# Attention and two MoE layers: the first part's order counts changes of TensorE's tiling, and the last tokens' step runs on column halves

## The chip, the cores and the metric

The kernel runs on one core of one Trainium2 chip. Its time is the device time of one execution, in microseconds. The engines are TensorE (PE; its weight loads are listed apart as PEld), VectorE (DVE), ScalarE (ACT), GpSimd (POOL) and the queue that issues most DMAs (SP).

## The reference

Three stages follow each other, all in 32-bit floating point. The first is attention by random features, for 4 batches of 8 heads with 576 tokens of 64 numbers; the second a dense layer pair over all 2304 tokens; the third a layer pair with 8 experts, of which each token takes one.

```python
def phi(x):                       # omega: 128 features of 64 numbers
    proj = einsum('bhsd,md->bhsm', x, omega)
    h = proj - sum(x * x, -1) / 2
    return exp(h - max(h)) / sqrt(128)
q_p, k_p = phi(q * scale), phi(k * scale)
kv = einsum('bhsm,bhsd->bhmd', k_p, v)
z = sum(k_p, axis=2)
attn = einsum('bhsm,bhmd->bhsd', q_p, kv) / (einsum('bhsm,bhm->bhs', q_p, z) + 1e-6)

x = attn, as 2304 tokens of 512
h = x @ w_in                      # 512 to 2048
x = max(0.01 * h, h) @ w_out      # 2048 to 512

expert = argmax(cosine(x, expert_emb) / tau)
out = gate * (max(x @ w1[expert], 0) @ w2[expert])
```

## The kernel before

The attention works on 16 pairs of heads. A pair has 2 x 512 tokens that fill the partitions four at a time, and the last 64 tokens of each head, which stand together as one tile of 128 partitions (the letter m in names). For each pair a chain of some 50 named steps runs over the engines. Its PE steps are:

- Tk, Tm, Tq: transposes of k, of the last tokens and of q (L516), on the full array.
- Pk, Pq: projections to features, one matmul for each head and tile, on 64 rows each: the array is tiled in two row halves (L532, form 64*128). Pm is the projection of the last tokens on the full array (L542).
- KVm, KV0, KV1: sums over tokens of features times values, one bank of PSUM (kv) for all three. The 128 features go out as two column halves of 64 (L597 and L607, form 128*64). KVm starts the sum with the last tokens; KV0 and KV1 add to it, in either order.
- F0, F1, Fm: transposes of q's features (L622, L626), full array.
- U0, U1: numerators and denominators, on column halves (L642; the last tokens at the end of U1, L649).
- XT: the finished x back into columns, four transposes (L688), full array. Xm: the same for the last tokens (L692), below.

Between them ACT, the DVE and POOL copy, square, take maxima and exponentials. After U0 and U1 the DVE's step dn (L661 to L664) takes the reciprocals of nine denominators, xs0 and xs1 (L671) divide, and xs1 also makes xm for the last tokens (L678). Of these, partitions 0 to 63 belong to one head and 64 to 127 to the other. The kernel before writes xm as 128 x 128 with zeros in the half that is the other head's: the multiply at L664 puts the reciprocal beside a zero, by a 0/1 mask named own, and L678 multiplies both copies. Xm then is one matmul of xm with two, the folded identity (both 64-column halves of the identity added up), made once at the start on POOL (L435 to L440).

As soon as pairs 0 to 3 are done, the dense layer's first group of five chunks (GROUPS[0], M1 and M2, L759 to L761 and L800 to L802) begins on the finished tokens, in blocks of 256, and fills PE beside the later pairs. The weights' conversion (steps C0 to CL) runs on the DVE, ACT and POOL beside it.

The order of all these steps, on every engine and in SP's queue of loads, is not left to the framework: issue_order plays the first part through in a small model, in which each entry of STEPS has, for each engine that could do it, a duration and a rank, its use of PSUM banks (+ takes, - gives back) and the steps before it. The rank of a step of pair i is its own plus RANK[0] times i (dense steps: RANK[2]). Where an engine is free, the step that can start first is taken, and among those that can start then, the one of lowest rank. The resulting list is emitted as it stands. Behind it, from the last attention step on, the framework orders the rest. BUSY is only the model's view of PE's clock.

Of the kernel before, what the change touches and what calls it, by code (L numbers as in the profile page):

```python
# [110 lines left out]
    "ylm": ("p", (("V", 0.14, 55.3),), "-xm", "yhm"),  # L111
# [21 lines left out]
}  # L133
RANK = (949.6, 44297.0, 875.5)
# [7 lines left out]
BUSY = {"KV0": 0.5, "KV1": 0.5, "KVm": 0.6, "U0": 0.5, "U1": 0.5}  # L142
# [3 lines left out]
def issue_order(dense):  # L146
# [41 lines left out]
    free["P"] = WARM  # L188

# [14 lines left out]
    while len(order) < len(waits):  # L204
# [6 lines left out]
        for e, steps in open_.items():  # L211
            at = {}
            for s in steps:
                at[s] = max(ready[s][e], free[e])
                b = kind_of_room(s)
                if b:
                    at[s] = max(at[s], spot(b)[0])
            soon = min(at.values(), default=math.inf)
            if soon < first:
                first, late = soon, soon + AHEAD[e]  # L220
                pick = min((rank[e, *s], s, e) for s in steps if at[s] <= late)[1:]
# [14 lines left out]
        if e == "P":  # L236
            work, dur = dur, 0.0
# [26 lines left out]
def tile_attention_moe_moe(  # L264
# [159 lines left out]

    v1s = [atp.tile([P, 5, 2, D + 2], F32, name=f"v1s{j}", tag=f"v1{j}") for j in range(2)]
    dns = [atp.tile([P, 11], F32, name=f"dn{j}", tag=f"dn{j}") for j in range(2)]
    xms = [atp.tile([P, P], F32, name=f"xm{j}", tag=f"xm{j}") for j in range(2)]
# [6 lines left out]

    own = atp.tile([P, 2], F32, name="own", tag="own")  # L435
    G.memset(own, 0.0)
    for h in range(2):
        G.memset(own[h * 64 : h * 64 + 64, h : h + 1], 1.0)
    two = atp.tile([P, D], F32, name="two", tag="two")
    G.tensor_tensor(two, ident[:, 0:D], ident[:, D:P], op=ALU.add)  # L440
# [160 lines left out]
    def kv(i, j):  # L601

        f = st[i].pop(f"fk{j}")
        for h in range(2):
            for a in range(2):
                for c in HALVES:
                    PE.matmul(  # L607
                        st[i]["kv"][c, h, :], f[:, 2 * h + a, c], vs[i][:, 2 * a + j, h, 0 : D + 1],
                        start=False, stop=(h == 1 and a == 1 and "kv_" in st[i]),
                    )  # L610
        st[i]["kv_"] = j
# [45 lines left out]
    def dens(i):  # L657


# [3 lines left out]
        V.reciprocal(dn[:, 0:9], dn[:, 0:9])  # L663
        V.tensor_scalar_mul(dn[:, 9:11], own, dn[:, 8:9])  # L664

    def ratio(i, j):
# [10 lines left out]
        if j == 1:  # L677
            V.tensor_tensor(  # L678
                xms[i % 2].rearrange("p (h d) -> p h d", h=2),
                u_view(i, 1)[:, 4:5, 0:D].to_broadcast([P, 2, D]),  # L680
                dn[:, 9:11].unsqueeze(2).to_broadcast([P, 2, D]), op=ALU.mult,
            )
# [34 lines left out]
    def on(f, *args):  # L717
        return lambda i, e: f(i, *args)
# [877 lines left out]
```

## Time and profile before

| | us |
|---|---|
| median of 3 runs | 835.98 (835.43 to 838.81) |
| the profiled execution | 839.26 |
| its span, first to last instruction | 837.5 |
| PE busy | 780.6 (93%) |
| DVE busy | 529.4 (63%) |
| ACT busy | 342.3 (41%) |
| POOL busy | 312.2 (37%) |
| granted clock of PE, mean | 0.980 |

The shares are means over parts that differ: the first part is attention with dense work beside it, then follow the rest of the dense layers and the experts. Busy time of PE counts matmuls from start to a modelled end, and they overlap; where the text below speaks of the cost of a step, it therefore goes from the start of one instruction to the start of the next.

### The profile page before, as it was taken

How to read it: one execution, taken by the hardware profiler on the slowest of the kernel's cores; microseconds unless marked ns; L12 is line 12 of the kernel's file. 1: busy time of each engine (PE TensorE's matmuls, PEld its weight loads, DVE VectorE, ACT ScalarE, POOL GpSimd, SP SyncE). 2: the span in 40 equal slices, each digit the busy share in tenths (PEclk: the TensorE clock that was granted, in tenths of full speed). 3: DMA queues.
4: the chain of work that ended last, by engine and by line, in shares of the span. 5: the costliest groups of instructions: out<-in, count | busy, mean ns of one | idle time of the engine just before them, and what ended most of it. 6: DMA issues, size and time to landing. Idle time of an engine off the chain costs nothing. (4 is left out here: it accounts for less than half of the span.)

```text
span 837.5 us, 15718 instructions
## 1 busy us (share of the span) xinstructions
PE 780.6 (93%) x5722; PEld 684.4 (82%) x5722; DVE 529.4 (63%) x1282; ACT 342.3 (41%) x878; POOL 312.2 (37%) x445
## 2 busy tenths in 40 slices
PE   7998999999999999999999999796978999998992
PEld 6776788888898999999989889675857789997992
DVE  6999987877465477253869789988894222222121
ACT  5885755766374444233333433542441211112110
POOL 5766543311064454244342443654562101111000
PEclk9999999999999999999999999898999899999997
DMA  5555423210263266351123412684631201111000
GB/s 157 158 137 139 136 75 102 62 41 16 76 228 129 76 217 220 131 190 36 55 46 45 47 39 39 213 124 117 67 99 26 66 26 53 51 51 51 26 26 31
DMA packets 68318, 75.85 MB, mean 91 GB/s; under 512 B 32691, under 2 KB 49148, under 8 KB 68094
## 3 DMA queue, kind: packets, MB, share of 16 engines
q1 hardware_dynamic: 64766, 65.19, 29.4%
q0 software_dynamic: 3456, 9.49, 3.7%
q8 instruction: 48, 0.79, 0.4%
q14 instruction: 48, 0.39, 0.2%
HBM read 55.65 MB, written 19.00 MB: 89 GB/s over the span
## 5 line engine op out<-in xcount | busy, mean ns | idle before, releaser
L320 POOL TENSOR_TENSOR glo<-gg,ghi 128x384 fp32r<-128x384 f32 (+1 forms) x97 | 101.6, 1048 | 185.2 <-ACT ghi L311 173.8
L759 PE MATMUL ph<-xb,ring 128*128 128x384 f32 (+1 forms) x444 | 142.0, 320 | 0.6 <-DVE ring L311 0.5
L760 PE MATMUL ph<-xb,ring 128*128 128x384 f32 (+1 forms) x444 | 140.2, 316 | 1.3 <-DVE ring L320 1.2
L761 PE MATMUL ph<-xb,ring 128*128 128x384 f32 (+1 forms) x444 | 140.6, 317 | 0.0
L934 DVE CUSTOM_DVE_ANT_0 jv<-xl,en 128x512 bf16<-128x512 f32 x144 | 124.9, 890 | 1.3
L800 PE MATMUL px<-ring,ghi 128*128 128x512 f32 x288 | 115.8, 402 | 7.3 <-ACT ghi L311 6.5
L801 PE MATMUL px<-ring,ghi 128*128 128x512 f32 x288 | 115.2, 400 | 0.2 <-DVE ring L320 0.2
L802 PE MATMUL px<-ring,glo 128*128 128x512 f32 x288 | 113.5, 402 | 1.3 <-POOL glo L320 1.3
L769 DVE SCALAR_TENSOR_TENSOR gg<-hs 128x384 f32<-128x384 f32 (+1 forms) x111 | 65.3, 589 | 75.9 <-ACT hs L311 71.1
L311 ACT CAST ghi<-gg 128x384 fp32r<-128x384 f32 (+1 forms) x104 | 49.0, 472 | 105.0 <-DVE gg L769 97.7
L759 PEld LDWEIGHTS ph<-xb,ring 128*128 128x128 f32 x444 | 84.1, 189 | 5.9 <-DVE ring L311 1.0
L760 PEld LDWEIGHTS ph<-xb,ring 128*128 128x128 f32 x444 | 84.0, 189 | 5.8 <-DVE ring L320 1.9
L761 PEld LDWEIGHTS ph<-xb,ring 128*128 128x128 f32 x444 | 84.1, 189 | 0.3
L1212 DVE SCALAR_TENSOR_TENSOR fh<-fh,fh 128x256 fp32r<-128x256 f32 x48 | 20.4, 425 | 90.6 <-ACT fh L1211 90.6
L311 ACT COPY hs<-ph 128x384 f32<-128x384 f32 (+1 forms) x101 | 44.0, 438 | 79.0 <-PE ph L761 76.2
L800 PEld LDWEIGHTS px<-ring,ghi 128*128 128x128 f32 x288 | 55.0, 191 | 16.9 <-ACT ghi L311 7.5
L802 PEld LDWEIGHTS px<-ring,glo 128*128 128x128 f32 x288 | 54.8, 192 | 14.7 <-POOL glo L320 2.8
L1211 ACT ACTIVATE fh<-fh 128x256 fp32r<-128x256 f32 x48 | 18.4, 384 | 112.8 <-PE fh L1205 112.7
L801 PEld LDWEIGHTS px<-ring,ghi 128*128 128x128 f32 x288 | 54.9, 191 | 9.0 <-DVE ring L320 0.5
L1278 POOL DMA_INDIRECT out_dram<-ot,xg x14 | 14.1, 1008 | 123.8 <-DVE ot L1277 79.5
L1203 PE MATMUL fh<-xth,w 128*128 128x256 f32 x128 | 35.8, 282 | 0.0
L1204 PE MATMUL fh<-xth,w 128*128 128x256 f32 x128 | 35.8, 281 | 0.0
(1085 smaller groups left out, 1743.5 us busy)
## 6 DMA issues: line engine op xcount, KB each, us to landing
xl<-xpart SPq DMA_DIRECT2D x36, 256.0 KB
rawi<-in_moe_w_in_dram SPq DMA_DIRECT2D x16, 512.0 KB
rawo<-in_moe_w_out_dram SPq DMA_DIRECT2D x16, 512.0 KB
rws<-in_moe_w_dram SPq DMA_DIRECT2D x16, 512.0 KB
xpart<-xo SPq DMA_DIRECT2D x18, 256.0 KB
xpart<-xl SPq DMA_DIRECT2D x18, 256.0 KB
xs<-xl SPq DMA_DIRECT2D x18, 256.0 KB
k<-in_k_dram SPq DMA_DIRECT2D x16, 256.0 KB
```

The source lines that it names most:

```text
L311: (A.copy if e == "A" else ENG[e].tensor_copy)(out_, in_)
L320: eng.tensor_tensor(lo, src, hi.bitcast(F32), op=ALU.subtract)
L759: PE.matmul(ph, wh, xb[blk][:, 0, kk, d], start=(kk == 0), stop=False)
L760: PE.matmul(ph, wl, xb[blk][:, 0, kk, d], start=False, stop=False)
L761: PE.matmul(ph, wh, xb[blk][:, 1, kk, d], start=False, stop=(kk == 3))
L769: V.scalar_tensor_tensor(gs["gg"], gs["hs"], 0.01, gs["hs"], op0=ALU.mult, op1=ALU.max)
L800: PE.matmul(px, ghi[:, d], r[:, 2, :], start=first, stop=False)
L801: PE.matmul(px, ghi[:, d], r[:, 3, :], start=False, stop=False)
L802: PE.matmul(px, glo[:, d], r[:, 2, :], start=False, stop=last)
L934: V.tensor_tensor_reduce(out=jv, in0=xfin[t], in1=rt["en"][:, e, :], scale=1.0, scalar=0.0, op0=ALU.mult, op1=ALU.add, accum_out=lg[:, j, ...
L1203: PE.matmul(ph, wh, xh, start=(kk == 0), stop=False)
L1204: PE.matmul(ph, wl, xh, start=False, stop=False)
```

## The change

All durations that a change of tiling had been mixed into are stated anew in STEPS, all ranks are others, and the order counts a change of tiling. KVm is no step of its own any more: it is issued at the head of KV0, and KV1 comes after KV0. Xm multiplies xm, now 128 x 64 without zeros, by the two column halves of the identity, each into its own 64 partitions of PSUM; own, two and the multiply at L664 go. Below, "..." stands for lines left out; every other line of STEPS has a new rank too.

```diff
-    "Lv": ("p", (("D", 2.5, 3363.9),), "", "KVm-2 KV0-2 KV1-2"),
+    "Lv": ("p", (("D", 2.5, -319.5),), "", "KV1-2"),
...
-    "Pk": ("p", (("P", 0.95, -1038.8),), "++pk", "xk"),
+    "Pk": ("p", (("P", 0.88, -1341.2),), "++pk", "xk"),
...
-    "Pq": ("p", (("P", 0.95, 693.6),), "++pq", "xq"),
+    "Pq": ("p", (("P", 0.88, 430.8),), "++pq", "xq"),
...
-    "KVm": ("p", (("P", 0.17, 521.8),), "+kv", "em Lv"),
-    "KV0": ("p", (("P", 0.7, -393.5),), "", "ek0 KVm"),
-    "KV1": ("p", (("P", 0.7, -489.4),), "", "ek1 KVm"),
-    "kf": ("p", (("A", 0.17, -142.9), ("V", 0.2, -1171.9)), "-kv", "KV0 KV1 U0-2 U1-2"),
+    "KV0": ("p", (("P", 0.69, -1008.2),), "+kv", "em Lv ek0"),
+    "KV1": ("p", (("P", 0.465, 162.4),), "", "ek1 KV0"),
+    "kf": ("p", (("A", 0.17, -686.0), ("V", 0.2, -1724.5)), "-kv", "KV1 U0-2 U1-2"),
...
-    "U0": ("p", (("P", 0.7, 1578.8),), "+u0", "fc0 kf"),
-    "U1": ("p", (("P", 0.85, -170.1),), "+u1", "fc1 fcm kf"),
-    "dn": ("p", (("V", 0.63, -194.0),), "", "U0 U1"),
+    "U0": ("p", (("P", 0.465, 1675.4),), "+u0", "fc0 kf"),
+    "U1": ("p", (("P", 0.58, 1455.6),), "+u1", "fc1 fcm kf"),
+    "dn": ("p", (("V", 0.46, 230.8),), "", "U0 U1"),
...
-    "xs1": ("p", (("V", 0.54, 1132.4),), "-u1", "dn XT-2 Xm-2"),
-    "XT": ("p", (("P", 0.44, -1465.1),), "+xt", "xs0 xs1"),
-    "Xm": ("p", (("P", 0.22, -3129.3),), "+xm", "xs1"),
+    "xs1": ("p", (("V", 0.47, 1587.0),), "-u1", "dn XT-2 Xm-2"),
+    "XT": ("p", (("P", 0.44, -1008.5),), "+xt", "xs0 xs1"),
+    "Xm": ("p", (("P", 0.116, -1036.3),), "+xm", "xs1"),
...
-    "M1": ("d", (("P", 1.4, -2103.9),), "+h", ""),
+    "M1": ("d", (("P", 1.4, 1419.6),), "+h", ""),
...
-    "M2": ("d", (("P", 1.38, 2123.8),), "+x", "GL"),
+    "M2": ("d", (("P", 1.38, 3751.0),), "+x", "GL"),
...
-RANK = (949.6, 44297.0, 875.5)
+RANK = (1003.0, 87777.0, 642.4)
...
-BUSY = {"KV0": 0.5, "KV1": 0.5, "KVm": 0.6, "U0": 0.5, "U1": 0.5}
+BUSY = {}
+
+HALVED = {"Pk": 1, "Pq": 1, "KV0": 2, "KV1": 2, "U0": 2, "U1": 2, "Xm": 2}
+CHANGE = 0.17
+SAME = 738.7
...
+    half = 0
...
-                pick = min((rank[e, *s], s, e) for s in steps if at[s] <= late)[1:]
+                pick = min(
+                    (rank[e, *s] - SAME * (e == "P" and HALVED.get(s[0], 0) == half), s, e)
+                    for s in steps if at[s] <= late
+                )[1:]
...
         if e == "P":
-            work, dur = dur, 0.0
+            work, dur = dur, CHANGE * (HALVED.get(name, 0) != half)
+            half = HALVED.get(name, 0)
...
-    dns = [atp.tile([P, 11], F32, name=f"dn{j}", tag=f"dn{j}") for j in range(2)]
-    xms = [atp.tile([P, P], F32, name=f"xm{j}", tag=f"xm{j}") for j in range(2)]
+    dns = [atp.tile([P, 9], F32, name=f"dn{j}", tag=f"dn{j}") for j in range(2)]
+    xms = [atp.tile([P, D], F32, name=f"xm{j}", tag=f"xm{j}") for j in range(2)]
...
-    own = atp.tile([P, 2], F32, name="own", tag="own")
-    G.memset(own, 0.0)
-    for h in range(2):
-        G.memset(own[h * 64 : h * 64 + 64, h : h + 1], 1.0)
-    two = atp.tile([P, D], F32, name="two", tag="two")
-    G.tensor_tensor(two, ident[:, 0:D], ident[:, D:P], op=ALU.add)
...
     def kv(i, j):
 
+        if j == 0:
+            kv_last(i)
         f = st[i].pop(f"fk{j}")
...
-                        start=False, stop=(h == 1 and a == 1 and "kv_" in st[i]),
+                        start=False, stop=(h == 1 and a == 1 and j == 1),
...
-        V.reciprocal(dn[:, 0:9], dn[:, 0:9])
-        V.tensor_scalar_mul(dn[:, 9:11], own, dn[:, 8:9])
+        V.reciprocal(dn, dn)
...
         if j == 1:
-            V.tensor_tensor(
-                xms[i % 2].rearrange("p (h d) -> p h d", h=2),
-                u_view(i, 1)[:, 4:5, 0:D].to_broadcast([P, 2, D]),
-                dn[:, 9:11].unsqueeze(2).to_broadcast([P, 2, D]), op=ALU.mult,
-            )
+            V.tensor_scalar_mul(xms[i % 2], u_view(i, 1)[:, 4, 0:D], dn[:, 8:9])
...
-        PE.matmul(ps[:, 0:D], xms[i % 2], two, start=True, stop=True)
+        for c in HALVES:
+            PE.matmul(ps[c, 0:D], xms[i % 2], ident[:, c], start=True, stop=True)
```

## Rows read from the trace of the kernel before

**Rows 1.** Busy time by stretch: stretch, busy us (instructions) of each engine, PE clock, DMA

```profile
20.00:112.00 92.00, 83.35 (x1036) 69.57 (x1032) 89.67 (x219) 67.33 (x214) 57.58 (x106) 1.00 0.50 136
112.00:220.00 108.00, 107.42 (x1315) 92.55 (x1315) 84.06 (x241) 66.28 (x213) 26.75 (x58) 1.00 0.19 55
220.00:500.00 280.00, 279.83 (x1507) 251.65 (x1506) 176.24 (x370) 113.57 (x246) 113.37 (x119) 1.00 0.39 115
500.00:838.00 338.00, 294.47 (x1714) 257.85 (x1712) 166.04 (x418) 85.01 (x183) 103.26 (x97) 0.95 0.29 66
```

**Rows 2.** PE in order of time (start, us, line, operation): first and last change

```profile
8.91 1.01 PE L532 MATMUL pj0k<-om_bd,x0k 64*128 64x128 f32 x5
...
215.91 0.50 PE L800 MATMUL px<-ring,ghi 128*128 128x512 f32 x1
```

**Rows 3.** PE in order of time, around a projection that stands alone

```profile
114.89 0.40 PE L801 MATMUL px<-ring,ghi 128*128 128x512 f32 x1
115.12 0.40 PE L802 MATMUL px<-ring,glo 128*128 128x512 f32 x1
115.45 1.16 PE L532 MATMUL pj7q<-om_bd,x7q 64*128 64x128 f32 x16
116.54 0.66 PE L516 MATMUL tr11k<-ident,k 128*128 128x128 f32 x4
```

**Rows 4.** PE in order of time: a U step alone, two projections together

```profile
189.00 0.69 PE L642 MATMUL u<-kvf,qT 128*64 128x65 f32 x16
189.61 0.66 PE L516 MATMUL tr15q<-ident,q 128*128 128x128 f32 x4
...
190.31 1.16 PE L532 MATMUL pj13q<-om_bd,x13q 64*128 64x128 f32 x16
191.30 1.06 PE L532 MATMUL pj15k<-om_bd,x15k 64*128 64x128 f32 x16
192.29 0.43 PE L692 MATMUL xpm<-two,xm 128*128 128x64 f32 x2
```

**Rows 5.** PE in order of time: both U steps of a pair in one visit

```profile
162.47 0.28 PE L760 MATMUL ph<-xb,ring 128*128 128x256 f32 x1
162.59 0.28 PE L761 MATMUL ph<-xb,ring 128*128 128x256 f32 x1
162.80 0.69 PE L642 MATMUL u<-kvf,qT 128*64 128x65 f32 x16
...
164.00 0.66 PE L516 MATMUL tr13q<-ident,q 128*128 128x128 f32 x4
```

**Rows 6.** PE in order of time, around an Xm between dense matmuls

```profile
104.63 0.33 PE L692 MATMUL xpm<-two,xm 128*128 128x64 f32 x2
104.77 0.36 PE L759 MATMUL ph<-xb,ring 128*128 128x256 f32 x1
104.97 0.28 PE L760 MATMUL ph<-xb,ring 128*128 128x256 f32 x1
```

**Rows 7.** Groups by line (busy us, mean ns): L664 in 20 to 112, 112 to 220

```profile
L664 DVE TENSOR_SCALAR dn<-own,dn 128x2 f32<-128x2 f32 x7 | 2.8, 403 | 0.2
...
L664 DVE TENSOR_SCALAR dn<-own,dn 128x2 f32<-128x2 f32 x9 | 2.4, 269 | 0.3
```

**Rows 8.** DVE in order of time, through the division of one pair

```profile
45.05 0.23 DVE L664 TENSOR_SCALAR dn<-own,dn 128x2 f32<-128x2 f32 x1
45.19 0.41 DVE L509 TENSOR_REDUCE ss<-sqs4k 128x8 f32<-128x256 f32 x1
...
46.81 0.28 DVE L678 TENSOR_TENSOR xm<-u,dn 128x128 f32<-128x128 f32 x1
47.01 0.21 DVE L509 TENSOR_REDUCE ss<-sqs4m 128x2 f32<-128x64 f32 x1
...
47.73 0.21 DVE L311 CAST xb<-xpm 128x64 fp32r<-128x64 f32 x1
47.86 0.41 DVE L549 TENSOR_REDUCE mx4m<-pj4m 128x2 f32<-128x256 f32 x1
```

More of the change, by code (lines that the diff above doesn't have):

```diff
@@ L52 @@
 STEPS = {
[58 rows of a table removed]
-    "ylm": ("p", (("V", 0.14, 55.3),), "-xm", "yhm"),
[21 rows of a table removed]
[57 rows of a table added]
+    "ylm": ("p", (("V", 0.14, 71.4),), "-xm", "yhm"),
[21 rows of a table added]
 }
-RANK = (949.6, 44297.0, 875.5)
+RANK = (1003.0, 87777.0, 642.4)
 LATE = {"P": 0.21, "A": 0.145, "V": 0.12, "G": 0.1, "D": 2.2}
@@ L608, in kv @@
                         st[i]["kv"][c, h, :], f[:, 2 * h + a, c], vs[i][:, 2 * a + j, h, 0 : D + 1],
-                        start=False, stop=(h == 1 and a == 1 and "kv_" in st[i]),
+                        start=False, stop=(h == 1 and a == 1 and j == 1),
                     )
-        st[i]["kv_"] = j
     def kv_copy(i, e):
@@ L727, in tile_attention_moe_moe @@
         "Tq": lambda i, e: trans(i, "q", qs[i].rearrange("p h t d -> p (h t d)")),
-        "KVm": on(kv_last), "kf": kv_copy, "dn": on(dens), "XT": on(x_trans_a),
+        "kf": kv_copy, "dn": on(dens), "XT": on(x_trans_a),
         "Xm": on(x_trans_m), "yh": by(x_hi, False), "yl": on(x_lo, False),
```

128 rows, old and new, of the table STEPS are left out of this document.

## The prediction

> **What bounds the kernel now.** The profile's page gives a span of 837.5 us with TensorE (PE) busy 93% of it; the profiled execution took 839.26 us, 3.28 above the median of the timed runs (835.98), so I make the sum against 839.26 and take 3.28 off at the end. The change sits in the first part alone, so the first view I read is busy time by stretch [rows 1]. Three regimes are to be seen there. From 20 to 112 us VectorE (DVE) is busy 89.67 of 92 us, 97%, and PE 83.35: PE idles 8.65 us, so the DVE sets the pace and PE work taken out there mostly turns into idle time. From 112 to 220 it is the other way round: PE 107.42 of 108, DVE 84.06. From 220 to 500 PE has 279.83 of 280, so whatever the first part ends earlier moves everything behind it forward, one for one. After 500 PE is down to 87% (294.47 of 338), waiting for things that hang on the end of the dense part; I let this tail move as a block.
>
> Next I read PE's rows in order of time, for what happens where the tiling of the array changes. The operand form says the tiling: 64*128 is the projections (two row halves), 128*64 the KV and U steps (two column halves), 128*128 all else. Going through all of them I count 137 changes of form in the first part, from the first projection at 8.91 us to the last return at 215.91 [rows 2]; 73 of them come after 112 us. They make up 30 visits to row halves and 44 to column halves, some of which touch.
>
> **What a change of tiling costs.** Row halves [rows 3, 4]: a dense step's matmuls start 0.23 us apart (114.89, 115.12), but the projection behind the last one starts 0.33 later, so entering costs 0.10. A projection alone takes 1.09 (115.45 to 116.54). The two that stand together, 190.31 and 191.30, take 1.00 and 0.99 up to 192.29. Two apart are thus 2 x (0.10 + 1.09) = 2.38, two together 0.10 + 1.99 = 2.09: one visit less saves 0.29. Column halves [rows 4, 5]: the first matmul starts 0.21 after the dense one ahead of it where 0.12 is usual, so 0.09 to enter. A U step of 16 matmuls alone takes 0.61 (189.00 to 189.61), both together with their 36 take 1.20 (162.80 to 164.00); the 20 more cost 0.59, 0.0295 each, so of the 0.61 some 0.47 are matmuls and 0.14 is the visit. One visit less saves 0.23. I take 0.13 for a change, half of the mean of 0.29 and 0.23; all 137 cost about 17.8 us of PE.
>
> **The change, part by part.** (1) The order. The planner now charges 0.17 us for each change and lets PE prefer a ready step of the tiling that it is in over one up to 738.7 ranks earlier; a pair of heads is 1003 ranks, so that is three quarters of a pair. KVm goes into KV0 and KV1 comes behind KV0, so that these two can be parted once at most. By the new ranks U1 and U0 of pair i stand at 1456 and 1675 and KV0 of pair i+2 at 998: less the 738.7 both U steps come right behind that KV0, where they are ready. Before, U1 stood at -170 and U0 at 1579, nearly two pairs apart. I expect the 44 column visits to become about 32 although Xm joins them, and the 30 row visits about 27: 15 visits or 30 changes less, 3.9 us. Both ends: no visit less (0) and 25 less (50 changes, 6.5 us). The matmuls are the same ones. The new order also moves each load, copy and conversion in its queue; no row of before says what that is worth, and 8.65 us of idle PE before 112 bounds the gain. I take 1.0 of it, since the DVE, not the order, accounts for most of that idle time, and bound the loss under the rivals.
>
> (2) Xm. Before, one full-array matmul (two instructions) against the folded identity: 104.63 to 104.77 is 0.14, and the dense matmul behind starts its successor after 0.20 instead of 0.12, so 0.22 in all [rows 6]. After, two column halves, four instructions of 64 columns; by the 0.0295 above they cost 0.12. Inside a column visit that is 0.10 less, 1.6 us over 16 pairs. Alone, each pays the visit: 0.12 + 0.23 - 0.22 = 0.13 more, 2.1 us worse over 16. Xm's rank (-1036) lets it go as soon as its data is there, which is some time after its own U steps, so it opens visits more than it joins them; but the preference then pulls waiting KV and U steps behind it. I take 12 joined and 4 alone: 1.2 - 0.5 = 0.7 us less.
>
> The Trainium skill, TensorEngine Tiling (Array Packing), Key Properties, says that changing the tiling mode, and not merely the tile, drains TensorE. The trace agrees with it by the 0.29 and 0.23 above. The rule speaks against this part: a step that ran in the mode of its neighbours is put into another one; taken alone it makes part (2) a loss of 2.1 us where I count a gain of 0.7.
>
> PE in sum: 3.9 + 0.7 = 4.6 us less (ends: 2.1 more to 8.1 less). Nine of 16 pairs have their ratio step after 112 us [rows 7], and 73 of the 137 changes lie there; 56% of 4.6, 2.6 us, falls where PE is the bound. The other 2.0 lies beside the DVE and I count it at nothing; if the DVE weren't the bound there it would be 2.0 more.
>
> (3) DVE. The multiply by "own" goes: its slot is 0.14 (45.05 to 45.19) [rows 8]. In the DVE-bound stretch it stands seven times with a mean of 403 ns [rows 7], so some of them were held far longer than this slot. The ratio of the last tokens writes 64 columns instead of 128: now 0.20 (46.81 to 47.01), afterwards about what a copy of 128x64 out of PSUM takes, 0.13 (47.73 to 47.86). That is 0.21 a pair, with ends of 0.14 (a pointer scalar makes the new one no shorter) and 0.47 (by the mean of 403). Seven pairs before 112: 1.5 us (1.0 to 3.3). The nine after 112 lie beside a full PE and count nothing.
>
> (4) GpSimd's making of "own" and "two" goes at the start, beside loads that the first transposes wait for: nothing.
>
> Sum: 2.6 + 1.0 + 1.5 = 5.1 us less. 839.26 - 5.1 = 834.2, and less the 3.28: **830.9 us**. What is late next: before 112 still the DVE, after it PE.
>
> **Rivals.** B, the DVE holds it all: the new order finds nothing in the 8.65 us and the joined visits fall mostly before 112; left are 1.5 of the DVE and 1.0 of PE, 2.5 less, 833.5. For it: 97% DVE; against it: 73 of the changes lie behind 112. C, the order gives more: with true prices for the projections and U steps the order stops feeding the DVE late, and half of the 8.65 goes as well as all 25 visits: 4.3 + 0.56 x (6.5 + 0.7) + 1.5 = 9.8 less, 826.2. For it: PE and DVE are both short of full in that stretch; against it: the DVE lacks only 2.33 us (92 - 89.67) there, so most of this must come from work handed to other engines. D, Xm makes its own visits, as by the rule above, and eats the grouping: 16 x 0.13 = 2.1 more against 3.9 less, 1.8 on PE, 1.0 of it behind 112, with 1.5 of the DVE and no gain of order: 2.5 less; with only 7 visits fewer (1.8 us), nothing is left of PE's part and it ends at 834.5. E, slower: PE stays in a tiling while a transpose or projection that feeds ScalarE and the DVE waits behind a visit of 1.20 us. The DVE has no slack before 112. If it runs dry for half of such a visit once a pair, that is 16 x 0.6 = 9.6 lost against 4.1 won (parts 1 to 3 without the 1.0): 5.5 more, 841.5. It decides from the point where the DVE's idle time in 20 to 112 grows from 2.3 us to beyond 6.5. Against it: a PE step is chosen only among those that are ready, and a preferred step is mostly 0.5 to 1.2 us long.
>
> **How the numbers follow.** A measurement of this kernel can tell about 0.5% from no change, 4.2 us: faster is below 831.8, slower above 840.2. Chances: forecast 0.44, B 0.18, C 0.12, D 0.12, E 0.14. The forecast lies 0.9 us inside the bound, so I give 0.40 of its 0.44 to faster; with C 0.52. Same: 0.04 + B + D = 0.34. Slower: E, 0.14. The forecast's own ends, put together, reach from 827.2 (0.56 x 8.1 + 3.3 + 1.0 = 8.8 less) to 836.2 (0.56 x 2.1 more, 1.0 of the DVE less, no gain of order: 0.2 more), which takes in B and D. To hold 8 in 10 the range must go past C (826.2), whose size is the least certain, and up to a mild E: 822 to 838.5.
>
> **What would show it.** Right: changes of form down from 137 to about 107; U0 and U1 together and KV0, U1, U0 in one visit; Xm beside KV or U in most pairs; the last pair's transposes some 5 us earlier than now; and PE still full from there to 500. The DVE stays at 95% or more before 112 but gets there sooner. Wrong: as many changes as before (D); the DVE with several us more idle time before 112, and PE rows that wait longer for copies (E); or a first part that does end 5 us earlier while the tail gives it back, which my sum doesn't hold.

## The result and the profile after

The changed kernel takes 826.23 us (median of 4 runs) against 835.7 before: a ratio of 0.9881, 95% interval 0.9857 to 0.9905, so 9.5 us less where 5.1 were forecast. A second set of runs gave 0.9883 (0.9859 to 0.9907). The sign and the range were right; the forecast was little over half of the gain. That the time is the one that rival C named is mostly luck: only part of it came by C's way.

The first part ends earlier and all else moves along. The first matmul of the dense layer's second group, the first of form 128x384, marks its end. In order of time on PE, before and after:

```profile
286.53 0.33 PE L759 MATMUL ph<-xb,ring 128*128 128x384 f32 x1
```

```profile
273.72 0.33 PE L755 MATMUL ph<-xb,ring 128*128 128x384 f32 x1
```

That is 12.81 us earlier in these two executions, whose spans differ by 12.6 (837.5 and 824.9): from there to the end they take 551.0 and 551.2. (The profiled execution of before was one of its longer ones, so 12.8 here stands for 9.5 in the medians.) So in these two executions the tail gives nothing back. How closely they agree is partly chance: in the twelve profiles of the runs below this stretch takes 546.3 to 549.9, so a few us given back or won there could not be told. Busy time by stretch of the changed kernel, columns as in [rows 1]:

```profile
20.00:112.00 92.00, 85.56 (x1108) 73.22 (x1105) 88.30 (x232) 72.55 (x227) 54.53 (x98) 1.00 0.51 138
112.00:220.00 108.00, 107.50 (x1323) 96.90 (x1322) 79.74 (x221) 61.84 (x200) 25.18 (x64) 1.00 0.19 55
220.00:500.00 280.00, 279.50 (x1491) 251.15 (x1490) 182.66 (x403) 115.99 (x249) 116.61 (x122) 1.00 0.40 115
500.00:838.00 338.00, 283.51 (x1649) 247.75 (x1648) 152.76 (x378) 78.55 (x169) 96.62 (x91) 0.94 0.27 64
```

From 20 to 112 PE is 2.2 us busier, the DVE 1.4 less, ACT 5.2 more. From 112 to 220 PE is as full as it was, 107.50 of 108, and yet does more: busy time can't show a gain that lies in the gaps between starts. In order of time on PE, one pair of the later part:

```profile
156.63 0.27 PE L516 MATMUL tr13m<-ident,m 128*128 128x128 f32 x1
156.83 0.44 PE L597 MATMUL kv<-v1s,f12m 128*64 128x130 f32 x4
157.10 0.64 PE L609 MATMUL kv<-v1s,f12k 128*64 128x65 f32 x16
157.57 0.64 PE L643 MATMUL u<-kvf,qT 128*64 128x65 f32 x16
158.04 0.29 PE L650 MATMUL u<-kvf,qT10m 128*64 128x65 f32 x4
158.15 0.64 PE L643 MATMUL u<-kvf,qT 128*64 128x65 f32 x16
158.62 0.64 PE L609 MATMUL kv<-v1s,f12k 128*64 128x65 f32 x16
159.19 1.16 PE L532 MATMUL pj11q<-om_bd,x11q 64*128 64x128 f32 x16
160.18 1.06 PE L532 MATMUL pj13k<-om_bd,x13k 64*128 64x128 f32 x16
161.17 0.34 PE L688 MATMUL xpm<-ident,xm 128*64 128x64 f32 x4
161.44 0.66 PE L683 MATMUL xp<-ident,xt 128*128 128x128 f32 x4
```

KV0 of pair 12, U1 and U0 of pair 10, KV1 of pair 12, both projections and Xm stand in one row without a full-array step between them: four changes of tiling for a pair, where before there were about eight. Counted over all rows of PE the changes fell from 137 to 98, and where they fell matters: up to 112 us 64 became 63, behind it 73 became 35.

To see what PE got done by a time, I add up its steps at the price that they have inside a visit, so without any change of tiling: a transpose 0.109, a projection 0.90, a KV or U matmul 0.0295, Pm 0.22 an instruction, dense ones 0.119 (M1) and 0.232 (M2), and Xm 0.12 in either form, so that the same steps count the same. By 112 us the kernel before had done 75.2 us of such work, the changed one 81.6; from 112 to 220 it was 93.5 and 100.6. That makes 6.4 and 7.1, 13.5 in all. (The four KV matmuls of the last tokens are twice as wide as the others; at twice the price the two become 6.6 and 6.9.)

### The profile page after: what moved, and what is told of

It is laid out like the page before. It is cut to its first block, busy times and chain, and to the rows that moved or that the text cites. A ratio compares the mean times of both kernels' runs of the same rounds, so it can differ in the third digit from the quotient of the medians.

```text
span 824.9 us, 15757 instructions
## 1 busy us (share of the span) xinstructions
PE 772.7 (94%) x5754; PEld 683.3 (83%) x5754; DVE 517.6 (63%) x1273; ACT 340.9 (41%) x876; POOL 306.0 (37%) x440
## 5 line engine op out<-in xcount | busy, mean ns | idle before, releaser
L328 POOL TENSOR_TENSOR glo<-gg,ghi 128x384 fp32r<-128x384 f32 (+1 forms) x93 | 98.4, 1059 | 165.7 <-ACT ghi L319 154.1
L930 DVE CUSTOM_DVE_ANT_0 jv<-xl,en 128x512 bf16<-128x512 f32 x144 | 122.7, 874 | 1.4
L765 DVE SCALAR_TENSOR_TENSOR gg<-hs 128x384 f32<-128x384 f32 (+1 forms) x111 | 63.4, 572 | 73.9 <-ACT hs L319 71.0
L319 ACT CAST ghi<-gg 128x384 fp32r<-128x384 f32 (+1 forms) x98 | 46.8, 478 | 96.5 <-DVE gg L765 91.0
```

The source lines that it names most:

```text
L319: (A.copy if e == "A" else ENG[e].tensor_copy)(out_, in_)
L328: eng.tensor_tensor(lo, src, hi.bitcast(F32), op=ALU.subtract)
L765: V.scalar_tensor_tensor(gs["gg"], gs["hs"], 0.01, gs["hs"], op0=ALU.mult, op1=ALU.max)
L930: V.tensor_tensor_reduce(out=jv, in0=xfin[t], in1=rt["en"][:, e, :], scale=1.0, scalar=0.0, op0=ALU.mult, op1=ALU.add, accum_out=lg[:, j, ...
```

## The experiments

Theory A is the prediction's: the DVE sets the pace before 112 us, and PE's time counts only behind it. Theory B lets PE's time count everywhere, theory C puts the gain into the new form of Xm; these letters are not those of the prediction's rivals. After the first four runs, theories G (the grouping carries the gain) and R (the new ranks do). Changes and work are counted as above; "old" and "new" form are those of the last tokens' step.

| run | changes to 112, 112 to 220 | work by 112, 112 to 220 | ratio to before (95%) |
|---|---|---|---|
| before | 64, 73 | 75.2, 93.5 | 1 |
| changed | 63, 35 | 81.6, 100.6 | 0.9881 (0.9857 to 0.9905) |
| changed, again | 63, 35 | 82.8, 100.5 | 0.9883 (0.9859 to 0.9907) |
| new form, old order | 73, 86 | 75.2, 92.7 | 0.9989 (0.9976 to 1.0001) |
| old form, new order | 55, 27 | 80.2, 100.8 | 0.9878 (0.9858 to 0.9899) |
| SAME = 0 | 87, 79 | 76.5, 92.8 | 0.9998 (0.9980 to 1.0016) |
| SAME from 112 on | 87, 42 | 77.0, 99.0 | 0.9947 (0.9922 to 0.9972) |
| SAME before 112 | 63, 73 | 81.9, 94.2 | 0.9921 (0.9895 to 0.9947) |
| rule, old ranks | 62, 55 | 75.2, 94.8 | 0.9996 (0.9980 to 1.0011) |
| new form for pairs 0 to 6 | 63, 27 | 82.1, 100.8 | 0.9868 (0.9849 to 0.9887) |
| new form for pairs 7 to 15 | 55, 35 | 80.2, 100.4 | 0.9875 (0.9856 to 0.9894) |
| PE work early | | | 1.0032 (1.0016 to 1.0047) |
| PE work late | | | 1.0087 (1.0069 to 1.0105) |
| DVE work early | | | 1.0138 (1.0114 to 1.0163) |

**The form alone, and the order alone.**

```diff
# the kernel before, its order kept
-        V.tensor_scalar_mul(dn[:, 9:11], own, dn[:, 8:9])
...
-        PE.matmul(ps[:, 0:D], xms[i % 2], two, start=True, stop=True)
+        for c in HALVES:
+            PE.matmul(ps[c, 0:D], xms[i % 2], ident[:, c], start=True, stop=True)
```

> Only the new form of the last tokens' step, in the order of the kernel before: changes of tiling 137 to 159. Theory A (the prediction's: the DVE sets the pace before 112 us, PE's time counts only behind it): 1.5 us less of the DVE, 0.56 x (16 x 0.13) = 1.2 more of PE, about 0.3 less than before. Theory B (PE sets the pace of the whole first part, since dense work fills what attention leaves, and the DVE's time counts nothing): 16 x 0.13 = 2.1 more than before. Theory C (the form carries the gain): 4 or more less.

> The new order with the old form of the last tokens' step (128 columns with zeros, one full-array matmul, the multiply by own on the DVE): changes 98 to 82. Against the changed kernel (826.2): theory A 1.5 more of the DVE and 0.56 x (1.6 - 2.1) = 0.3 less of PE, 1.2 more; theory B 0.5 less; theory C 4 or more longer.

The form alone gives 0.9989, an interval that touches no change; the order alone, with the old form and the reverse of this diff, 0.9878, all of the gain that an interval of 0.2% each way can show. Theory C falls. B's 1.0025 for the form alone lies outside its interval, A's 0.9996 inside; for the order alone both (0.9895 and 0.9875) fit.

**PE work and DVE work put into the kernel before.**

```diff
             PE.transpose(ps[:, 0:P], st[i]["fm"][:, 0, :], ident)
+            if 0 <= i < 8:              # late: 8 <= i < 16
+                for _ in range(9):
+                    PE.transpose(ps[:, P : 2 * P], st[i]["fm"][:, 0, :], ident)
...
-        V.reduce_sum(ss, s_...)         # the DVE's run, alone
+        for _ in range(4 if part == "q" and 0 <= i < 8 else 1):
+            V.reduce_sum(ss, s_...)
```

> The kernel before with nine more transposes (0.109 us each, into an unused part of the same bank) behind Fm of pairs 0 to 7, all before 112 us: 7.8 us more PE work. Theory A: 0 to 2 us longer than before, since PE idles 8.65 us there. Theory B: 7 to 8 us longer.

> The same nine transposes behind Fm of pairs 8 to 15, behind 112 us: 7.8 us more PE work where PE is full. Both theories: 7.8 us longer than before.

> The kernel before with the sum of squares of q (L509, 0.33 us a slot) made four times instead of once in pairs 0 to 7: 7.9 us more DVE work before 112 us, none elsewhere. If the DVE sets the pace there, as predicted: 7 to 8 longer. If PE does: 0 to 1. If they share it as the run with more PE work there says (0.43 of it counted): about 4.5.

Against a before of 833.93 the early PE work costs 2.7 us of 7.8 by its ratio (3.4 by the medians), the late 7.3. Behind 112 PE's time counts nearly in full, before it between a third and a half; B falls. The 7.9 of the DVE cost 11.5 (0.0138 x 834.79), more than was put in. Busy time by stretch, first with PE's early work, then with the DVE's:

```profile
20.00:112.00 92.00, 87.32 (x1090) 75.39 (x1090) 87.91 (x216) 65.49 (x207) 56.37 (x102) 1.00 0.48 131
```

```profile
0.00:20.00 20.00, 15.81 (x123) 13.03 (x123) 12.29 (x34) 9.35 (x22) 9.54 (x63) 0.83 0.59 166
20.00:112.00 92.00, 75.99 (x980) 63.08 (x981) 88.15 (x218) 60.69 (x192) 53.31 (x105) 0.96 0.45 123
```

In the first PE's busy time before 112 goes from 83.35 [rows 1] to 87.32: part of the extra work lies in what was idle time. In the second the DVE is no busier than before, but PE falls from 83.35 to 75.99, and its granted clock to 0.96 there and 0.83 in the first 20 us (1.00 and 0.91 in the profiled execution of before). So the DVE does set the pace before 112, as A has it, but A's zero for PE's time there is too low. The clock stood at 0.50, the lower of its two levels, for 13.6 us before 112, against 3.4 in before's profile. The 10.2 us more are worth up to 5.1 us at full clock, enough for the 3.6 by which the cost exceeds the 7.9; that they are its cause no run shows.

**The preference and the ranks.**

```diff
-SAME = 738.7
+SAME = 0.0
# and, with SAME = 738.7, the preference from 112 on, or before it
-                    (rank[e, *s] - SAME * (e == "P" and HALVED.get(s[0], 0) == half), s, e)
+                    (rank[e, *s] - SAME * (first >= 112 and e == "P" and HALVED.get(s[0], 0) == half), s, e)
```

> The changed kernel with SAME = 0: the same new ranks, durations and form, the order without the preference for the tiling PE is in; 170 changes instead of 98, 53 of the 72 more behind the projection of pair 9. Theory G (the grouping carries the gain, 0.15 us a change in full behind that point and 0.43 of it before): 9.1 more than the changed kernel, about 0.999 of before. Theory R (the new ranks carry it, whatever the tiling): at most 3 more, about 0.991 of before.

> The kernel before with the new form, the new durations of PE and the rule for tilings (SAME = 550, CHANGE = 0.17), but its own ranks: 115 changes instead of the 159 of the first experiment, 37 of the 44 fewer behind the projection of pair 9. Theory G: 5.8 less than that experiment, about 0.992 of before. Theory R: no gain, 0.999 of before.

> The changed kernel once more, beside the others of this group: 0.988 of before.

> The changed kernel with the preference for the tiling PE is in only from 112 us on (of the order's own clock): 131 changes, 80 before the projection of pair 9 and 51 behind it (changed kernel: 61 and 37). If a change costs 0.16 us of PE in full behind 112 and less than half of that before: 14 x 0.16 + 19 x 0.16 x 0.43 = 3.5 more than the changed kernel, 0.9925 of before. If the early grouping is what moves attention forward: the first part is as late at 112 us as without any preference, 5 us of work behind, and the time is 0.996 or more.

> The changed kernel with the preference only before 112 us: 137 changes, 61 before the projection of pair 9 (as in the changed kernel) and 76 behind it. Late grouping at 0.16 us a change in full: 39 x 0.16 = 6.2 more than the changed kernel, 0.9958 of before, and as much work done at 112 us as in the changed kernel. If the late changes are hidden: 0.989.

Without the preference the changed kernel is back at before (0.9998), as G forecast and R did not. Only late, it keeps 0.53% of the 1.17%; only early, 0.79%: the two add up to 1.32%, within their intervals the whole. Late grouping as forecast would have left the early-only run at 0.9958; its interval ends just below. But with the old ranks the rule gives nothing (0.9996 against 0.9989 for the same form without it), though changes fall from 159 to 117: here G failed. (That run has SAME = 550, KVm as a step of its own, and the new durations of dn and xs1 too, so it differs from the changed kernel in more than its ranks.) SAME = 0 has KVm in KV0 and KV1 behind it, so with these ranks this too gains nothing by itself. Late-only was also to tell whether the early grouping is what moves attention forward. At 112 us it is 4.6 us of work behind the changed kernel, as that reading had it; its interval holds the times of both readings, 0.9925 and 0.996. Busy time by stretch of the run with the old ranks:

```profile
20.00:112.00 92.00, 82.63 (x1050) 69.19 (x1049) 86.52 (x215) 68.19 (x216) 53.57 (x110) 0.98 0.48 134
112.00:220.00 108.00, 105.89 (x1332) 92.75 (x1331) 77.07 (x233) 67.39 (x212) 23.91 (x50) 1.00 0.19 52
```

PE idles 2.1 us behind 112, against 0.6 before [rows 1], and the DVE is down to 86.52 ahead of it: I read this as preferred steps making others late, rival E's mechanism in a smaller size. The clock is a second candidate: in this execution it stood at half for two stretches of 3.4 us before 112 (the 0.98), and no run separates the two. Neither the rule nor these ranks alone are faster; they are so together. Whether other ranks would gain without the rule, no run tries.

Early-only and late-only show where the gain lies. Busy time of the early-only run:

```profile
20.00:112.00 92.00, 85.65 (x1105) 73.30 (x1104) 88.46 (x233) 72.58 (x226) 54.36 (x98) 1.00 0.49 137
112.00:220.00 108.00, 107.33 (x1281) 92.03 (x1279) 76.42 (x214) 62.71 (x203) 22.74 (x49) 1.00 0.18 54
```

It is the changed kernel up to 112 (81.9 of work, 81.6) and the kernel before behind it, in its count of changes (73) and nearly in its work (94.2; 93.5 there, whose nine Xm cost 0.10 more each). So 6.6 us of the gain (0.79%, 4.4 to 8.8) come with as many changes as before (63 and 73 against 64 and 73), and by the work done they come before 112.

With the new form, work behind 112 follows the count of changes: 92.7 at 86, 94.2 at 73, 99.0 at 42, 100.4 to 100.6 at 35. From 73 to 35 that is 6.3 us for 38 changes, 0.16 each. With the old form there it is 93.5 at 73 and 100.8 twice at 27: 7.3 for 46, 0.16 again, on a line some 0.8 lower. Below their line lie SAME = 0 (by 0.4) and the old ranks with the rule (by 2.4), the two runs with over 1 us of idle PE there. In time the late changes show less than in work. From early-only to the changed kernel it is 0.38%, 3.2 us, where the work says 6.3; from SAME = 0 to late-only 0.51%, 4.3 us, where it says 6.2. Each ratio is uncertain by 0.2 to 0.25%, so the full price is at the edge of the first interval and inside the second; the late PE work, of which 7.3 of 7.8 us counted, speaks for the full price.

Ahead of 112 there is no such line: 63 changes go with 81.6 to 82.8 of work, 64 of the kernel before with 75.2, 87 with 76.5 and 77.0. Part of that is the clock. In the SAME = 0 run (busy time by stretch, the last three numbers are granted clock, DMA share and GB/s):

```profile
100.40:103.80 3.40, 1.63 (x23) 1.20 (x22) 3.33 (x12) 2.13 (x9) 1.28 (x4) 1.00 0.39 87
103.90:107.20 3.30, 3.30 (x18) 3.30 (x17) 1.90 (x6) 1.85 (x6) 0.62 (x3) 0.50 0.12 27
```

PE is busy 1.63 of 3.40 us, while the DVE is full, and then it runs at 0.50 of its clock for 3.4 us: a stall of 1.8 us is followed by half of 3.4, another 1.7 lost by my estimate. The late-only run, whose order up to there is the same, has it too; the changed kernel has full clock at the same place:

```profile
99.00:102.40 3.40, 1.76 (x35) 1.31 (x30) 3.33 (x11) 1.76 (x7) 2.02 (x4) 1.00 0.36 82
102.50:105.80 3.30, 3.27 (x13) 3.09 (x14) 2.31 (x7) 2.26 (x7) 0.76 (x3) 0.50 0.14 32
```

```profile
103.90:107.20 3.30, 3.30 (x30) 3.30 (x29) 3.27 (x7) 2.56 (x8) 2.34 (x3) 1.00 0.41 107
```

Such stretches of 3.4 us before 112 stand in the profiles of before (one), the new form in the old order (one), SAME = 0 (two), late-only (one), the rule with old ranks (two) and the DVE's work (four); the other eight have none. The one of before lies at the start:

```profile
8.10:11.40 3.30, 3.30 (x21) 2.75 (x21) 1.64 (x5) 1.87 (x3) 0.00 (x0) 0.50 0.27 74
```

There it isn't always so: the run with late PE work, whose order is the same up to 112, has none, and 76.3 of work by then. Of the 6.4 us at 112 some 1.1 (76.3 - 75.2) to 1.7 (half of 3.4) is therefore this stretch of one execution, which the medians hold only in part; that is a third to a half of the 3.3 us by which the ends of the first part differ more (12.8) than the medians (9.5). Where the rest of these 3.3 us lies, no run tells.

**The form by stage.**

```diff
-            V.tensor_scalar_mul(xms[i % 2], u_view(i, 1)[:, 4, 0:D], dn[:, 8:9])
+            if i < 7:                   # the counterpart: i >= 7
+                V.tensor_scalar_mul(xms[i % 2][:, 0:D], u_view(i, 1)[:, 4, 0:D], dn[:, 8:9])
+            else:
+                V.tensor_tensor(...)    # as before, with own; and in Xm likewise
```

> The changed kernel, its order kept, with the new form of the last tokens' step for pairs 0 to 6 and the old form for pairs 7 to 15: 90 changes. The form saves DVE time, which counts before 112 us, and costs changes, which count behind it: about 1.2 less than with the new form everywhere, 0.987 of before, with the work at 112 us as in the changed kernel and more of it done from 112 to 220. If the form matters nowhere: 0.988.

> The counterpart: old form for pairs 0 to 6, new form for pairs 7 to 15, 90 changes. It has the DVE's cost early and the changes' cost late: about 1.2 more than the changed kernel, 0.990 of before. If the form matters nowhere: 0.988.

With the new form early, 82.1 of work is done by 112, with the old one 80.2; the whole kernels agree (81.6 and 82.8 against 80.2). From 112 to 220 the old form has 100.8, the new one 100.4 to 100.6. So by the work done the form gains some 2.0 us where the DVE sets the pace (1.4 to 2.6; two executions of the changed kernel alone differ by 1.2), even with eight more changes there, and loses 0.2 to 0.4 where PE does: Xm costs 0.10 less, 0.9 for nine pairs, and its eight changes 1.3 more. The sum, under 2 us, is less than the first pair of runs could see. The times (0.9868 and 0.9875, 823.11 and 824.27 us) lie in the expected order, but their intervals overlap, and the 0.990 expected for the counterpart lies just outside its own: the times don't show what the work does. The new form for pairs 0 to 6 alone has the lowest ratio of all runs and isn't proved faster than the changed kernel.

## Why the prediction fell short

What bounds the kernel was read rightly: PE behind 112 (7.3 of 7.8 us counted), mostly the DVE before it, and a tail that moves as a block, within the 5 us by which it varies. That fewer changes of tiling gain time was right too, but it is only a part of the gain. Two terms of the sum 2.6 + 1.0 + 1.5 were too small:

- "30 changes less, 3.9 us" and "56% of 4.6, 2.6 us, falls where PE is the bound". Measured are 39 less, of which 38 lie behind 112, at 0.16 each: 6.1, and with the nine Xm there (0.10 each) 7.0 of the 7.1 us of work from 112 to 220, where the sum has 2.6. The times show 3.2 us of it (early-only against changed).
- "I take 1.0 of it", for what the new order does beside the changes. Early-only has the count of changes of before and is 6.6 us shorter, where the sum has 2.5 for the order and the DVE together. In time this is the larger miss. By what the order gains there is settled only in part, as said below.

In detail:

- *The count and its place.* I took each saved change from a saved visit. The visits fell by 11 only: the column visits from 44 to 40, 13 of them Xm alone, which leaves 27 for KV and U, and the row visits from 30 to 23 (27 forecast). The rest is that visits now touch: 28 changes go directly between row and column halves, where before 11 did. I also spread the saving over the first part as the changes of before are spread, but before 112 the count stayed (64 and 63). Not that nothing can be joined there: the preference takes 24 changes away (87 without it, 63 with it). But without it the new ranks and form have 23 more than before, eight of them by the form (55 and 63).
- *The price.* 0.13 left out what the steps behind a visit lose. I compare each slot, from start to start, with its step's price (the wide KV matmuls at twice theirs), over all 14 profiles from 112 to 220. The slot ahead of a change is longer by 0.09 into halves, and by 0.12 to 0.15 out of them or directly from one kind to the other; the next five instructions together lose another 0.02 to 0.06 (medians). The work by stage says 0.16 for all of it, and a direct change between row and column halves counts as one. The Trainium skill, TensorEngine Tiling (Array Packing), Key Properties, says that changing the tiling mode drains TensorE. The trace agrees in that each change costs time, whichever two modes it lies between.
- *Xm.* 12 joined and 4 alone was wrong: of 16, three share a visit with KV or U. But ten stand next to a projection, nine of them right behind it as at 161.17, where they cost one change and not two; in the new order, old form against new is 82 and 98 changes, one a pair. Over 16 pairs that is 2.6 us of changes against 1.6 of Xm's own: a loss of 1.0 for PE where I counted a gain of 0.7. Rival D had the direction of this part and twice its size (2.1); that Xm would eat the grouping did not come.
- *The DVE.* The multiply by own went (dn takes 8.4 us of the DVE in the first part instead of 13.6). Three of its 16 instructions, of 577 to 893 ns, were held as I said, and the trace shows by what: they end when an instruction of GpSimd ends, here at 82.3:

```profile
81.28 1.04 POOL L498 TENSOR_TENSOR sqs8k<-k 128x512 f32<-128x512 f32 x1
81.45 0.89 DVE L664 TENSOR_SCALAR dn<-own,dn 128x2 f32<-128x2 f32 x1
```

  But the slot of the new multiply is no shorter than the one of before [rows 8], by the DVE's rows in order of time:

```profile
40.18 0.74 DVE L670 TENSOR_TENSOR xt<-u,dn 128x256 f32<-128x256 f32 x2
40.84 0.28 DVE L677 TENSOR_SCALAR xm<-u,dn 128x64 f32<-128x64 f32 x1
41.03 0.68 DVE L399 SCALAR_TENSOR_TENSOR tti<-rawi,tti 128x512 int32<-128x512 int32 x1
```

  0.19 from start to start, for 64 columns as for 128: the lower end that I gave. The 1.5 us stand nonetheless by the work done: the form is worth some 2.0 before 112.
- *The order before 112.* I gave 1.0. With the form's 2.0 taken off, and 1.1 to 1.7 for the clock, 2.7 to 3.3 of the 6.4 are left. The preference there gives 0.77% between SAME = 0 and early-only, more than 24 changes at full price (3.8 us, 0.46%), and PE's time counts only in part there. Its profile is also without the two stretches of half clock of SAME = 0. The bias steps (L566) take 9.3 us of the DVE in the first part instead of 12.8. That is hardly work handed to others (43 instructions instead of 47; 15 fewer for q, 11 more for the rest) but mostly fewer held ones: three of over 500 ns, 2.4 us, instead of seven, 5.4 us. How the rest divides between ranks and preference isn't settled, and so the cause of this part stays open.
- *Rivals.* B and D's times are excluded by the interval, E by its sign, though its mechanism may have shown where the ranks were left as they were. C's time came about, by half its way: the largest part of C's 9.8 was to be half of PE's idle time (4.3), and PE idles 6.44 instead of 8.65 us, 2.2 less.

## What to carry to other kernels

Price a change of TensorE's tiling like an instruction and count it by stage: here nearly all were saved where PE is the bound. Count direct changes too, since visits that touch save one each. An order can also gain at an unchanged count: most of the time gained here came so. When an order is written out by hand, a rule for grouping and the priorities under it belong together; tried alone, each of them gave nothing here. A step that saves one engine's time at another's cost can be worth it in one stage and not in the next, and a sum over the kernel hides both.

## What the runs showed of the hardware

- A change of tiling costs 0.16 us of PE's work where PE is the bound (6.3 us for 38), a direct one between row and column halves included.
- A stall of PE of 1.8 us was followed by 3.4 us at half clock, in both runs that had that order. Work put on the DVE before 112 cost 1.46 times itself (11.5 for 7.9 us), in an execution with 13.6 us of half clock there.
- Small DVE instructions were held by GpSimd: over all 14 profiles, each of the 79 multiplies by own and bias steps that lasted over 500 ns (0.15 to 0.23 us is usual) ended 0.02 to 0.04 us after a TENSOR_TENSOR that had been running on POOL when it started; of the 631 under 300 ns, 48 ended so.
- A DVE multiply by a pointer scalar out of PSUM takes a slot of 0.19 us for 64 columns, as the two-tensor one did for 128 (0.20).
